# Sparse attention and an MLP on one core: products of zeros in TensorE's empty stretches, a third buffer of gathered values, two raw slots of the first weight, and a new order

## The chip, the cores and the metric

The kernel runs on one core of a Trainium2 chip, in one launch. The metric is device time in microseconds (us) from the start of the launch to its end; the number of a kernel is the median of several executions. The profile is of one execution. PE is TensorE, DVE is VectorE, ACT is ScalarE, POOL is GpSimd, and SP is SyncE, which here only issues DMA transfers.

## What is computed

Block-sparse attention over 4 batches, 8 heads, 768 positions and head size 64, and behind it a two-layer MLP over the 3072 tokens. A query block of 32 positions sees its own and both neighbouring key blocks, the first and the last block, and three sampled blocks; the first and the last query block see all keys. Cut down, the reference is:

```python
mask = abs(blk_i - blk_j) <= 1                      # 24 blocks of 32 positions
mask |= (blk_i == 0) | (blk_j == 0) | (blk_i == 23) | (blk_j == 23)
for qb in range(24):
    for kb in sampled_blocks[qb]:                   # three per query block
        mask[rows of qb, columns of kb] = True
attn = softmax(where(mask, q @ k.T / 8, -1e9)) @ v
x = attn, heads side by side                        # 3072 x 512
h = x @ w_in                                        # 512 x 2048
g = h * tanh(softplus(h))
out = g @ w_out                                     # 2048 x 512
```

Both weights arrive as 64-bit floats and are brought to a pair of f16 values (a high and a low part) on the chip.

## The kernel before, in words

**The jobs.** Each batch has 13 attention jobs: eleven pairs of query blocks, each block with gathered keys and values, and two dense jobs (first and last query block). They are numbered through from 0 to 51. A job is a chain over the engines: `s` (scores, PE, L633 for batch 0 and L643 for the others), `mx` (row maximum, DVE, L686), `nb` (L699 or L701), `pt` (exponentials, ACT, L712), `t` (transposes, PE, L732), `pp` (back to SBUF, ACT and DVE), `o` (product with the values, PE, L777 or L787), `r` and `xs` (division, DVE, L808 to L813), `tx` (transpose, PE, L820), `xh` and `xl` (two f16 parts, ACT and DVE, L838 and L841). Batch 0 is computed in f32, the others in pairs of f16.

**The gathers.** The values of a batch are written to a table in DRAM (`vd`, L527). For each query block SP issues transfers of the window (L590), of rows of zeros at the ends (L593) and of the three sampled blocks (L596) into a buffer `vg`. There are two such buffers (`NVG`), used in turn; a gather into a buffer waits until the `o` that reads it is done. Sampled keys are copied by POOL (`kg`, L574).

**The weights.** `w_in` comes in eight pieces of 1 MB into a ring of three raw slots (`wr`, L857). A piece is decoded by three DVE instructions (L865, L868, L871), then PE takes its squares (`gram_wi`, L357), and when two pieces are there a scale is found (`tp_w`, L381, and `ws`), and each piece is split into its high part (`wi`, L926) and low part (L929). `w_out` comes in sixteen pieces of 0.5 MB (`wor`) into the ring `raw` of six slots, which the raw tiles of Q, K and V of the coming batches use as well. It is decoded by the same three lines, squared (`gram_wo`), given one scale for all (`tp_wo`, L383), and split (L963, L966, L968).

**The MLP.** It works on twelve tiles of 256 tokens, three for each batch. A tile has 16 steps `h` of 12 products of 128x256 (L1007), taken from PSUM by ACT (`hs`, L1016), the activation on ACT, DVE and POOL (L1030 to L1051), and 16 steps `y` of 6 products of 128x512 (L1066). The first `h` step of a batch's first tile needs the jobs 0 to 4, and its split weights. The PSUM ring `h` has two slots; the squares of `w_in` use it too.

**The order.** Nothing of this is ordered by hand or at run time. Each step is added to a plan with an estimated length, what it reads and writes, which ring slots it takes, and a number (`key=`). `Plan.emit` walks through time, takes for each engine the step that could begin first, among those within 0.02 of each other the one with the lowest ready time plus `key`, and emits it. On an engine the instructions then run in that order, each waiting for its inputs, and whatever is behind a waiting instruction on the same engine waits as well. `pace` holds back the `s` of a job: the first eighteen by a list of earliest times (`START`), the later ones by how much of the MLP is done (`RES`).

Of the kernel before, what the change touches and what calls it, by code (L numbers as in the profile page):

```python
# [10 lines left out]
F16 = mybir.dt.float16  # L11
BF16 = mybir.dt.bfloat16
I32 = mybir.dt.int32
AF = mybir.ActivationFunctionType
# [11 lines left out]
RINGS = dict(s=1, t=2, o=1, h=2, y=1, raw=6, wr=3, pt=2, pp=4, xh=3, xl=3, mx=3, nb=3, r=2,  # L26
# [14 lines left out]
class Plan:  # L41
# [42 lines left out]

    def emit(self, pace):
# [16 lines left out]
        while todo:  # L102
# [30 lines left out]
            start, t, took, t.eng = best  # L133
            for e in t.ways:
                ready[e].remove(t)
# [42 lines left out]
def attn_mish_kernel(ctx: ExitStack, tc: tile.TileContext, qT, kT, v, sampled, blocks, w_in, w_out, out):  # L178
# [134 lines left out]
    NKG, NVG = 2, 2  # L313
# [45 lines left out]
    def add_gram(key, srcs, keys, ring, out, w, new_, cls):  # L359
# [7 lines left out]
        for n, k in enumerate(keys):  # L367
            add("PE", 0.45 if ring == "y" else 0.8, lambda n=n: fn(n), r=[k], w=[kg], new=[(ring, kg)] if n == 0 else (),
                key=cls + 3, lat=0.25)
# [4 lines left out]
        add("DVE", 0.4, diag, r=[kg], w=w, new=new_, key=cls - 7)  # L374
# [20 lines left out]
    def add_root(key, ss, fn, r, after, w, new, cls, n=1, apart=False):  # L395

        add("PE", 0.3 * n, lambda: root_pe(key, ss(), apart), r=r, w=[key], new=[("t", key)], key=cls + 4, lat=0.3)
        add("DVE", 0.6, fn, r=[key, *after], w=w, new=new, key=cls - 23)

    def load32(what, j):  # L400
# [4 lines left out]
        def fn():  # L405
# [5 lines left out]
            key=-23, lat=1.8, kind=("dma", 4.4 if what == "k" else 1.5, 1))  # L411

    def load(b, what, js, ring="raw", after=()):
# [3 lines left out]
        def fn():  # L417
# [12 lines left out]
            new=[(ring, key) for key in keys], key=-5 if b == 0 else 0, lat=1.8,  # L430
            kind=("dma", 1.5 * n, n))

    def sums(b, what, j, cls):
# [7 lines left out]
        add("ACT", 1.28, fn, r=[("raw", what, b, j)], w=[key], new=[(f"ss{what}", key)] if first else (), key=cls + 87)  # L441
# [24 lines left out]
    def parts(b, what, j, cls):  # L466
# [32 lines left out]
        if what == "v":  # L499
            add("POOL", 0.5, ends, w=[("ends",) + key], r=[kr], new=[("raw", key)], use=[key], key=cls - 5)  # L500
# [3 lines left out]
            use=use + ([key] if what != "k" else []), key=cls - 22)  # L504
        add("DVE", 1.3, lo, port=True, r=[kr, ks, kh], w=[key, ("done",) + key], use=use, key=cls + 3)

    def copy_v(j):
# [14 lines left out]
        add("POOL", 0.3, ends, w=[("ends",) + key], new=[("raw", key)], use=[key], key=21)  # L522
        add("DVE", 0.8, lambda: fn("DVE"), r=[kr, ("ends",) + key], w=[key], use=[key], key=ATV + 53,
            also=[("ACT", 1.16, lambda: fn("ACT")), ("POOL", 2.0, lambda: fn("POOL"))])

    def store_v(b, j):
        add("SP", 0.9, lambda: nc.sync.dma_start(  # L527
            out=vd[b][j * TT:(j + 1) * TT].rearrange("(c p) h d -> p c h d", p=P), in_=tl["v", b, j]),
            r=[("v", b, j)], w=[("vd", b, j)], key=37, lat=1.8, kind=("dma", 1.7, 1))
# [4 lines left out]
    def globals_(b):  # L534
# [5 lines left out]
        for n in range(NKG):  # L540
            add("POOL", 1.0, lambda n=n: fn(n), r=KT3(b), w=[("kg", n)], use=[("kt", b)], key=-7)

    def globals_v(b, n):
# [3 lines left out]
        add("SP", 0.9, fn, r=VD3(b), w=[("vg", n)], key=-1, lat=1.8, kind=("dma", 0.5, 2))  # L547
# [19 lines left out]
    def gather_k(su):  # L567
# [7 lines left out]
        add("POOL", 1.3, fn, r=KT3(b) + ["off"], w=[("kg", n)], use=[("kt", b)], key=10)  # L575
        if su["whole"]:
            add("DVE", 0.5, lambda: nc.vector.tensor_copy(  # L577
                out=kgs[n][:, :, 0:WK], in_=tl["kt", b][:, :, (qb - 1) * BS:(qb + 2) * BS]),
                r=KT3(b), w=[("kw", n)], use=[("kt", b)], key=-12)

    def gather_v(su):
# [15 lines left out]
        add("SP", 2.3, fn, r=VD3(b) + ["off", "z"], w=[("vg", n)], key=-16, lat=1.8, kind=("dma", 1.1, NR + 1 + (a0 > 0) + (a1 < WK)))  # L597

    def fetch_dense(su):
# [11 lines left out]
        for j in T3:  # L611
# [3 lines left out]
                key=8, lat=1.8, kind=("dma", 1.7, 1))  # L615
# [32 lines left out]
    def attend(job):  # L648
# [9 lines left out]
        def s_fn():  # L658
# [17 lines left out]
            use=[("kt", b)], key=104, lat=0.25, kind=("S", i))  # L676
# [12 lines left out]
        add("DVE", 2.6 if dense else 1.27, mx_fn, r=[ks] + (k2 if dense else []), w=[kmx], new=[("mx", kmx)], key=10.5)  # L689
# [4 lines left out]
        def nb_fn(eng):  # L694
# [9 lines left out]
            new=[("nb", ("nb", i))], key=-1.5, also=[("DVE", 0.35 * len(wq), lambda: nb_fn("DVE"))])  # L704
# [50 lines left out]
        for j in range(nt):  # L755
            kj = ("t", i, j)
            add("PE", 0.48, lambda j=j: t_fn(j), r=[("p", i, j // 2 if dense else j)], w=[kj, "t in order"], new=[("t", kj)], use=kps,
                key=10, lat=0.25, kind=("T", i))
            kpp = ("pp", i, j)
            if exact(b):  # L760
                add("ACT", 0.62, lambda j=j: pp_fn(j, "ACT"), r=[kj], w=[("ph", i, j), ("pl", i, j)], use=[kpp],
                    new=[("pp", kpp)], key=-2.5, also=[("DVE", 0.72, lambda j=j: pp_fn(j, "DVE"))])
                continue
            add("ACT", 0.62, lambda j=j: ph_fn(j), r=[kj], w=[("ph", i, j)], new=[("pp", kpp)], use=[kpp], key=-29.5)
# [515 lines left out]
```

## Time and profile before

| what | value |
|---|---|
| median of 3 runs | 774.58 us (773.07 to 776.49) |
| the profiled execution | 773.79 us |
| its span, first to last instruction | 772.0 us |
| PE busy, share of the span | 93% |
| DVE, ACT, POOL busy | 63%, 68%, 41% |
| bytes moved by DMA | 94.08 MB |

The span lies 1.8 us under the profiled execution's own time. A row of the timeline gives the start, the length, the engine, the line, the operation with the tile that it writes and those that it reads, and in brackets how long the engine had stood idle before it and for whom. The window view gives for each stretch the busy time of each engine, then the clock that PE was granted (1.00 is full), the share of time that the 16 DMA engines were busy, and GB/s. The chain of waits is followed back from the last instruction, at each step to what released it.

### The profile page before, as it was taken

Reading aid. Unit: us, or ns where it says so; the run is one execution under the profiler, and the core shown is the slowest. Engines: PE = TensorE matmul, PEld = TensorE weight load, DVE = VectorE, ACT = ScalarE, POOL = GpSimd, SP = SyncE. Lnnn points to the kernel's source line nnn. Section 1 sums busy time; section 2 is a strip of 40 time slices with the busy share of each in tenths; the row PEclk is TensorE's granted clock in tenths of the full one; section 3 lists DMA queues with packets and bytes.
Section 4 is the critical chain, followed back from the end, with each engine's and each line's share of the span. In section 5 each row is a group of like instructions: output and inputs, shape, how many; then the busy total and the mean of one; then the engine's idle time right before and its main releaser. Section 6 shows DMA issues by size and latency. Waiting matters only on the chain.

```text
span 772.0 us, 27811 instructions
## 1 busy us (share of the span) xinstructions
PE 714.2 (93%) x11766; PEld 501.7 (65%) x11766; DVE 486.2 (63%) x868; ACT 523.9 (68%) x811; POOL 314.1 (41%) x402
## 2 busy tenths in 40 slices
PE   2765888899999999999999999999999999999997
PEld 1554666565777666766677767677676676666663
DVE  3877988987867755767667767877766642323230
ACT  4455767888867777876677868777777665555650
POOL 2168531685436434434534534344551522213021
PEclk9768999999999999999999999999999999999999
DMA  7899796212524555154245643534333330000000
GB/s 274 303 279 231 219 261 211 82 43 98 180 59 119 159 142 154 66 167 117 58 113 143 180 138 103 160 89 127 99 86 93 117 88 15 14 15 14 14 15 28
DMA packets 55905, 94.08 MB, mean 122 GB/s; under 512 B 8035, under 2 KB 18788, under 8 KB 55780
## 3 DMA queue, kind: packets, MB, share of 16 engines
q1 hardware_dynamic: 55584, 92.03, 40.4%
q8 instruction: 93, 1.52, 0.9%
q14 instruction: 32, 0.26, 0.1%
q10 hardware_dynamic: 196, 0.27, 0.1%
HBM read 79.32 MB, written 12.95 MB: 120 GB/s over the span
## 4 chain that ended last, share of the span: by engine, by line
PE 78%; DMA 10%; DVE 6%; ACT 2%; issue 2%; SPq 1%; POOL 1%; POOLq 0%; ACTq 0%; DVEq 0%
PE y L1066 30%; PE h L1007 29%; DMA vg<-vd 7%; PE t L732 6%; PE o L787 5%; PE s L643 4%; PE tx L820 1%; PE o L777 1%; DMA q<-in_q_dram 1%; PE s L633 1%; POOL wo L968 1%; DMA wr<-in_moe_w_in_dram 1%; ACT pt L712 1%; DVE q L492 1%; DVE kg L577 1%
## 5 line engine op out<-in xcount | busy, mean ns | idle before, releaser
L1007 PE MATMUL h<-xh,wi 128*128 128x256 f16 x1536 | 282.4, 273 | 3.0 <-issue 1.6
L1066 PE MATMUL y<-wo,g 128*128 128x512 f16 x1152 | 277.9, 379 | 1.5 <-POOL g L1051 0.9
L1007 PEld LDWEIGHTS <-wi 128*128 128x128 f16 x2304 | 222.7, 98 | 54.3 <-issue 6.9
L1007 PE MATMUL h<-xl,wi 128*128 128x256 f16 x768 | 209.3, 273 | 0.2 <-issue 0.2
L1051 POOL TENSOR_TENSOR g<-hs,g 128x1024 f16<-128x1024 f32 x48 | 104.3, 2173 | 252.7 <-DVE g L1048 143.6
L1066 PEld LDWEIGHTS <-g 128*128 128x128 f16 x1152 | 110.6, 98 | 102.6 <-issue 3.7
L574 POOL COPY kg<-kt 128x256 f16 (+1 forms) x264 | 108.1, 453 | 88.0 <-PE s L643 57.0
L1016 ACT ACTIVATE hs<-h,gsc 128x512 f32<-128x512 f32 x96 | 65.6, 686 | 77.4 <-PE h L1007 77.4
L712 ACT ACTIVATE pt<-s,nb,ns 128x256 f32<-128x256 f32 (+1 forms) x208 | 104.5, 580 | 1.4 <-DVE nb L701 0.4
L1040 DVE SCALAR_TENSOR_TENSOR hs<-us,hs 128x1024 f32<-128x1024 f32 x48 | 60.6, 1263 | 53.4 <-ACT us L1039 53.3
L732 PE MATMUL t<-ident,pt 128*128 128x128 f32 x448 | 73.4, 288 | 9.3 <-ACT pt L712 8.4
L749 ACT ACTIVATE pp<-t 128x512 f16<-128x512 f32 x84 | 49.8, 595 | 39.6 <-PE t L732 38.7
L752 DVE SCALAR_TENSOR_TENSOR pp<-t,pp 128x512 f16<-128x512 f32 x84 | 57.1, 684 | 28.8 <-ACT pp L749 28.5
L732 PEld LDWEIGHTS t<-ident,pt 128*128 128x128 f32 x448 | 53.5, 146 | 21.7 <-issue 7.8
L1036 POOL TENSOR_TENSOR us<-us 128x1024 f32<-128x1024 f32 x20 | 38.6, 1932 | 60.9 <-DVE us L1034 50.8
L686 DVE TENSOR_REDUCE mx<-s 128x4 f32<-128x1024 f32 x44 | 53.3, 1212 | 6.4 <-PE s L643 3.8
L1030 ACT ACTIVATE us<-hs,hsc 128x1024 f32<-128x1024 f32 x48 | 55.2, 1150 | 1.2
L1038 ACT ACTIVATE us<-us 128x1024 f32<-128x1024 f32 x48 | 50.7, 1056 | 4.4 <-POOL us L1036 3.6
L1039 ACT ACTIVATE us<-us 128x1024 f32<-128x1024 f32 x48 | 50.8, 1058 | 1.0
L1034 DVE TENSOR_SCALAR us<-us 128x1024 f32<-128x1024 f32 x48 | 35.9, 747 | 22.6 <-ACT us L1030 22.3
L1048 DVE CAST g<-hs 128x1024 f16<-128x1024 f32 x37 | 28.9, 781 | 26.2 <-PE y L1066 25.6
L787 PEld LDWEIGHTS <-pp 128*32 128x32 f16 x4032 | 37.2, 94 | 12.0 <-issue 9.2
(188 smaller groups left out, 788.4 us busy)
## 6 DMA issues: line engine op xcount, KB each, us to landing
vg<-vd SPq DMA_DIRECT2D x304, 65.0 KB, 2.3
vg<-vd SPq DMA_DIRECT2D x80, 195.0 KB, 3.3
wr<-in_moe_w_in_dram SPq DMA_DIRECT2D x8, 1024.0 KB, 8.9
wor<-in_moe_w_out_dram SPq DMA_DIRECT2D x16, 512.0 KB, 4.4
vd<-v SPq DMA_DIRECT2D x12, 520.0 KB, 5.7
raw_v<-in_v_dram SPq DMA_DIRECT2D x12, 512.0 KB, 5.8
out_dram<-ys SPq DMA_DIRECT2D x24, 256.0 KB, 2.1
raw_k<-in_k_dram SPq DMA_DIRECT2D x9, 512.0 KB, 5.8
```

The lines of the kernel that those rows point to most:

```text
L574: nc.gpsimd.tensor_copy(out=kg[n][:, :, c0:c0 + BS], in_=kt[:, :, ds(j, BS)])
L686: nc.vector.tensor_reduce(out=mx.rearrange("p g w -> p (g w)"), in_=tl[ks].rearrange("p g (w k) -> p (g w) k", k=KT), axis=AX.X, op=ALU.max)
L712: ex = lambda o, x, g, w: nc.scalar.activation(out=o, in_=x, func=AF.Exp, bias=nb[:, g, w:w + 1], scale=ns(w)[:, 0:1])
L732: nc.tensor.transpose(t[:, k, g], src, ident)
L752: nc.vector.scalar_tensor_tensor(out=tl["pl", i, j], in0=tl["t", i, j], scalar=PSC, in1=tl["ph", i, j], op0=ALU.mult, op1=ALU.subtract)
L787: nc.tensor.matmul(o[cs, w, g, 0:v1 - v0], p[:, k, g, cs], vt[:, k, 2 * c + g, v0:v1], start=j == 0 and g == 0 and k == 0 and n == 0, stop ...
L1007: nc.tensor.matmul(h[:, f2].rearrange("p (s q) -> p s q", q=BS), wi[:, fp, w, cc, fs], x[:, :, cc], start=f2 == 0 and k == 0, stop=f2 == 1 ...
L1016: nc.scalar.activation(out=tl[kq][:, 2 * (fp % 2):2 * (fp % 2) + 2], in_=tl[kh], func=AF.Copy, scale=gsc[:, fp:fp + 1])
L1030: nc.scalar.activation(out=new(sb, "us", ku, [P, 4, TT]), in_=hs(), func=AF.Exp, scale=hsc[:, b:b + 1])
L1040: add("DVE", 1.32, lambda: nc.vector.scalar_tensor_tensor(out=hs(), in0=us(), scalar=-0.5, in1=hs(), op0=ALU.add, op1=ALU.mult), r=[ku], w ...
L1051: add("POOL", 2.3, lambda: nc.gpsimd.tensor_tensor(out=g()[:, 1], in0=hs(), in1=g()[:, 0], op=ALU.subtract), r=[kq, ("gh", b, t, k)], w=[k ...
L1066: nc.tensor.matmul(tl[ky], tl["g", b, t, k][:, g, f, q], wo[:, fc, w], start=fc == 0 and n == 0, stop=fc == NFC - 1 and n == 2)
```

## The change

Four things are changed.

- **Products of zeros.** `Plan.emit` looks, whenever it puts a step on PE whose estimated start lies between 3 and 150, at the estimated gap ahead of it. If it is over 0.5, it first emits `int((gap - 0.3) / 0.24)` matmuls of a 128x128 tile of zeros with itself, 512 columns wide (L860 in the changed kernel), into a PSUM tile that nobody reads. That tile is one of the two slots of the ring `h`, and is given back when job 8 (`LAST`), the ninth, begins. 97 such products are emitted.
- **A third `vg` buffer** (`NVG` 3). The dense job of a batch then has all three parts of its values in `vg`, and takes no slot of `raw`.
- **Two raw slots** of `w_in` in place of three.
- **The order.** Nearly all `key=` numbers, `START` and `RES` have other values.

```diff
-RINGS = dict(..., raw=6, wr=3, ...)
+RINGS = dict(..., raw=6, wr=2, ...)
...
+    zeros = None
+    FROM, TILL = 3.0, 150
...
             start, t, took, t.eng = best
+            idle = start - free.get("PE", 0.0)
+            if t.eng == "PE" and self.zeros and self.FROM < start < self.TILL and idle > 0.5:
+                self.zeros(int((idle - 0.3) / 0.24))
...
-    NKG, NVG = 2, 2
+    NKG, NVG = 2, 3
...
-            new=[(ring, key) for key in keys], key=-5 if b == 0 else 0, lat=1.8,
+            new=[(ring, key) for key in keys], key=(-5 if b == 0 else 0) + 90, lat=1.8,
...
+    z16 = const.tile([P, P], F16, name="z16")
+    nc.gpsimd.memset(z16, 0.0)
+    spare = []
+
+    def zeros(n):
+        for _ in range(n if spare else 0):
+            nc.tensor.matmul(spare[0].rearrange("p (n q) -> p n q", q=P), z16, z16.unsqueeze(1).to_broadcast([P, 4, P]),
+                             start=True, stop=True)
+
+    plan.zeros = zeros
...
+    LAST = 8
...
+    add("PE", 0.0, lambda: spare.append(new(ps["h"], "h", ("zeros",), [P, 512])), w=["zeros"], new=[("h", ("zeros",))],
+        key=-999)
...
+        if i == LAST:
+            add("PE", 0.0, spare.clear, r=["zeros", ("begun", i)], use=[("zeros",)], key=-1035)
...
-    RES, START = 1611, [82, 15, 81, 0, 10, 49, ...]
+    RES, START = 453, [218, 93, 2, 128, 14, 40, ...]
```

Three places show how instructions move. The first is SP at the first gathers. `wr` is a piece of `w_in`, `vg` a buffer of gathered values, `vd` the table in DRAM; L546 fetches the two fixed blocks, L590 opens a gather with the window. Before:

```order
L857 DMA wr_3_361<-in_moe_w_in_dram 128x4x512
L546 DMA vg0_111<-vd0_60 32x520 x2
L546 DMA vg1_112<-vd0_60 32x520 x2
L857 DMA wr_4_505<-in_moe_w_in_dram 128x4x512
L590 DMA vg0_111<-vd0_60 64x520
L593 DMA vg0_111<-vd0_60 32x520
```

The same place in the changed kernel:

```order
L873 DMA wr_4_544<-in_moe_w_in_dram 128x4x512
L552 DMA vg0_111<-vd0_60 32x520 x2
L552 DMA vg1_112<-vd0_60 32x520 x2
L552 DMA vg2_113<-vd0_60 32x520 x2
L873 DMA wr_5_657<-in_moe_w_in_dram 128x4x512
L596 DMA vg0_111<-vd0_60 64x520
L599 DMA vg0_111<-vd0_60 32x520
```

The first gather stood behind the piece with the number 4 and stands behind number 5 now; with two slots that piece waits until number 3 is decoded, as number 4 with three slots waited for number 1. Ahead of all this the two first pieces of `w_in` now stand before the three loads of V of batch 0, where they stood behind them. The second place is SP further on. Before, behind the fifth gather, the loads of K of batch 1 come (`raw_k_1`, three slots of `raw`):

```order
L596 DMA vg0_111<-vd0_60 32x520
L426 DMA raw_k_1_0_929<-in_k_dram 128x4x256
L426 DMA raw_k_1_1_931<-in_k_dram 128x4x256
L426 DMA raw_k_1_2_933<-in_k_dram 128x4x256
L590 DMA vg1_112<-vd0_60 96x520
```

In the changed kernel nothing but gathers stands between the eighth piece of `w_in` and the ninth gather, and behind that come pieces of `w_out` (`wor`):

```order
L602 DMA vg2_113<-vd0_60 32x520
L873 DMA wor_0_1277<-in_moe_w_out_dram 128x1024
L873 DMA wor_1_1296<-in_moe_w_out_dram 128x1024
L873 DMA wor_2_1304<-in_moe_w_out_dram 128x1024
L873 DMA wor_3_1346<-in_moe_w_out_dram 128x1024
L596 DMA vg0_111<-vd0_60 96x520
```

The loads of K and of the first Q of batch 1 have moved behind all sixteen pieces of `w_out`, the last of which stands nine SP rows ahead of the first of them. The third place is PE among the first jobs: `s_2` are the scores of job 2, `t_1` and `t_2` the transposes of jobs 1 and 2. Before:

```order
L732 MATMUL t_1_0_398<-ident_64,pt_1_372 128x128 x4
L732 MATMUL t_1_1_408<-ident_64,pt_1_372 128x128 x4
L820 MATMUL tx_0_416<-ident_64,xs_0_406 128x128
L633 MATMUL s_2_421<-kt_0_120,q_0_0_154 32x96 x8
L633 MATMUL s_2_421<-kg0_109,q_0_0_154 32x160 x8
```

In the changed kernel:

```order
L639 MATMUL s_2_477<-kg1_110,q_0_0_158 32x160 x8
L826 MATMUL tx_0_516<-ident_64,xs_0_513 128x128
L738 MATMUL t_1_0_534<-ident_64,pt_1_440 128x128 x4
L860 LDWEIGHTS z16_118
L860 MATMUL zeros_123<-z16_118 128x512
L860 LDWEIGHTS z16_118
L860 MATMUL zeros_123<-z16_118 128x512
L738 MATMUL t_1_1_553<-ident_64,pt_1_440 128x128 x4
```

The scores of job 2 went ahead of the transposes of job 1, and two products of zeros stand between those. 33 stand ahead of the first scores, 24 between these and the squares of the first piece of `w_in`, and the other 40 in 17 groups of one to five up to the start of job 8.

More of the change, by code (lines that the diff above doesn't have):

```diff
@@ L373, in diag @@
                                            accum_out=out())
-        add("DVE", 0.4, diag, r=[kg], w=w, new=new_, key=cls - 7)
+        add("DVE", 0.4, diag, r=[kg], w=w, new=new_, key=cls + 492)
     def root_pe(key, ss, apart):
@@ L395, in add_root @@
     def add_root(key, ss, fn, r, after, w, new, cls, n=1, apart=False):
[L397 to L398 removed]
+        add("PE", 0.3 * n, lambda: root_pe(key, ss(), apart), r=r, w=[key], new=[("t", key)], key=cls + 3, lat=0.3)
+        add("DVE", 0.6, fn, r=[key, *after], w=w, new=new, key=cls + 12)
     def load32(what, j):
@@ L440, in fn @@
             squares(tl["raw", what, b, j], tl[key][:, k:k + 1])
-        add("ACT", 1.28, fn, r=[("raw", what, b, j)], w=[key], new=[(f"ss{what}", key)] if first else (), key=cls + 87)
+        add("ACT", 1.28, fn, r=[("raw", what, b, j)], w=[key], new=[(f"ss{what}", key)] if first else (), key=cls - 74)
     def scales(b, what, j, cls):
@@ L499, in parts @@
         if what == "v":
-            add("POOL", 0.5, ends, w=[("ends",) + key], r=[kr], new=[("raw", key)], use=[key], key=cls - 5)
+            add("POOL", 0.5, ends, w=[("ends",) + key], r=[kr], new=[("raw", key)], use=[key], key=cls + 11)
         kh = ("hi",) + key
@@ L521, in fn @@
                 (nc.vector if eng == "DVE" else nc.gpsimd).tensor_copy(out=dst, in_=src)
-        add("POOL", 0.3, ends, w=[("ends",) + key], new=[("raw", key)], use=[key], key=21)
-        add("DVE", 0.8, lambda: fn("DVE"), r=[kr, ("ends",) + key], w=[key], use=[key], key=ATV + 53,
+        add("POOL", 0.3, ends, w=[("ends",) + key], new=[("raw", key)], use=[key], key=-2)
+        add("DVE", 0.8, lambda: fn("DVE"), r=[kr, ("ends",) + key], w=[key], use=[key], key=ATV - 63,
             also=[("ACT", 1.16, lambda: fn("ACT")), ("POOL", 2.0, lambda: fn("POOL"))])
@@ L977, in fn @@
             nc.vector.tensor_scalar(out=gsc, in0=iv_i, scalar1=rg, scalar2=-2.0 * GSC, op0=ALU.mult, op1=ALU.mult)
-        add("DVE", 0.7, fn, r=[("iv", k) for k in range(0, NFP, 2)], w=["gsc"], key=-14)
+        add("DVE", 0.7, fn, r=[("iv", k) for k in range(0, NFP, 2)], w=["gsc"], key=21)
     def scales_b(b):
```

90 lines of the change are left out of this document (45 added, 45 removed).

## The prediction

> **What bounds the kernel now.** I read the page first:
>
> ```profile
> span 772.0 us, 27811 instructions
> PE 714.2 (93%) x11766; PEld 501.7 (65%) x11766; DVE 486.2 (63%) x868; ACT 523.9 (68%) x811; POOL 314.1 (41%) x402
> ```
>
> PE is busy for 93% of the span, so over most of it a shorter wait elsewhere is worth nothing. Time can come only from the 57.8 us in which PE stands (772.0 - 714.2) and from where its clock is low. The window view says where that is; its columns are PE, weight loads, DVE, ACT, POOL, granted clock, DMA share and GB/s:
>
> ```profile
> 0.00:20.00 20.00, 6.03 (x102) 3.09 (x103) 7.56 (x26) 8.30 (x13) 5.61 (x26) 1.00 0.80 279
> 20.00:83.00 63.00, 44.31 (x924) 32.87 (x923) 50.57 (x96) 34.78 (x66) 34.81 (x49) 0.76 0.93 268
> 83.00:200.00 117.00, 103.00 (x1515) 74.85 (x1514) 101.11 (x158) 90.77 (x133) 62.26 (x60) 1.00 0.52 151
> 200.00:640.00 440.00, 433.39 (x8402) 309.79 (x8400) 295.93 (x552) 324.68 (x531) 184.89 (x256) 1.00 0.41 118
> 640.00:772.00 132.00, 127.47 (x832) 81.08 (x830) 31.04 (x37) 65.39 (x70) 26.50 (x12) 1.00 0.05 17
> ```
>
> PE stands for 14.0 us up to 20, 18.7 up to 83, 14.0 up to 200, and then 6.6 and 4.5; the clock is low from 20 to 83 alone. I cut at 83 because there the MLP begins, whose steps can fill PE. Three rows of PE's timeline, the second query block of job 1, that of job 4, and the first `h` product:
>
> ```profile
> 48.61 0.90 PE L777 MATMUL o<-vg,pp 128*32 128x65 f32 x32
> ...
> 78.06 0.66 PE L777 MATMUL o<-vg,pp 128*32 128x65 f32 x32
> ...
> 82.91 0.27 PE L1007 MATMUL h<-xh,wi 128*128 128x256 f16 x1
> ```
>
> What holds that up is in the chain of waits, in order of time:
>
> ```profile
> 40.41 7.62 DMA vg<-vd
> 48.05 6.61 DMA vg<-vd
> ...
> 63.49 7.60 DMA vg<-vd
> ...
> 72.49 1.89 PE s L633 x64
> ```
>
> From 40 to 71 nearly everything on the path is gathers: each goes out when an `o` has freed its buffer, and the next `o` waits for it to land. That is the stage in which a third buffer matters. In 20 to 83 DVE is the busiest engine, with 50.57 of 63 us, and stands for 12.4.
>
> **The gathers.** From 48.61 to 78.06 six query blocks pass, 4.9 us each, with two buffers in flight. With three, at the same latency, it is two thirds, 3.3 us, and six take 19.6 instead of 29.5: 9.8 us less. Is there bandwidth? The issue view has the sizes and the time to landing:
>
> ```profile
> vg<-vd SPq DMA_DIRECT2D x304, 65.0 KB, 2.3
> vg<-vd SPq DMA_DIRECT2D x80, 195.0 KB, 3.3
> wr<-in_moe_w_in_dram SPq DMA_DIRECT2D x8, 1024.0 KB, 8.9
> ```
>
> A gather is 195 + 3x65 = 390 KB, six are 2.3 MB, and two pieces of `w_in` go with them: 4.4 MB, at 268 GB/s 16 us, under 19.6. DVE allows up to 12.4 us, if it stood no more. It also waits less by its order: the decode of the last piece now stands ahead of job 3's division, behind which it stood:
>
> ```profile
> 72.55 0.22 DVE L808 TENSOR_SCALAR r<-o,iv_r 128x4 f32<-128x4 f32 x1 [3.06 <-PE o L777]
> ...
> 73.36 1.21 DVE L871 SCALAR_TENSOR_TENSOR wi<-wr,wi 128x1024 int32<-128x1024 int32 x1
> ```
>
> I take 9 us, with the ends 0 and 12.4. V of batch 0 now lands behind 2 MB of `w_in`, 7.5 us later at 279 GB/s, and with it the table that the gathers read. I cost that at nothing: before, the first gather was not held by V but stood on SP behind a piece of `w_in` that waited for a slot.
>
> ```profile
> 35.08 0.39 SPq L857 DMA_DIRECT2D wr<-in_moe_w_in_dram  x1
> 35.50 0.61 SPq L590 DMA_DIRECT2D vg<-vd  x1
> ```
>
> In the new order it stands behind another such piece, whose slot should come at about the same 35 to 40 us, since decoding begins earlier. Without that cover it costs up to 5 us.
>
> **Two slots of `w_in`.** A slot goes through landing (8.9 us) and decode (two DVE steps of 1.22 and a shorter one), about 12 us, so two slots give a piece every 6 us. From some 16 us on, the eighth is there at about 64, and the last decode before ended at 74.6. Nothing, while the gathers end later than that; if they don't, this is the next to be late.
>
> ```profile
> L868 DVE SCALAR_TENSOR_TENSOR wi<-wr,wi x8: 1207/1218/1941, 21.6 to 68.0; 128x1024 int32<-128x1024 int32 x8
> ```
>
> **K behind `w_out`.** By the tiles `raw_k` and `wor`, K of batch 1 was loaded at 58.8 and not taken until 175.2, and `w_out` was issued from 71.1 to 131.7:
>
> ```profile
> L426 SPq DMA_DIRECT2D raw_k<-in_k_dram x9: 413/505/1250, 58.8 to 421.5; - x9
> L488 ACT ACTIVATE kt<-raw_k,sc_k x9: 1132/1133/1151, 175.2 to 470.7; 128x1024 f16<-128x1024 f32 x9
> ...
> L857 SPq DMA_DIRECT2D wor<-in_moe_w_out_dram x16: 327/363/1582, 71.1 to 131.7; - x16
> L871 DVE SCALAR_TENSOR_TENSOR wo<-wor,wo x16: 677/692/710, 80.5 to 137.9; 128x512 int32<-128x512 int32 x16
> ```
>
> For all that time three of the six `raw` slots were taken, and `w_out` went through what was left. Now all are free for it, 2 MB less stands ahead of it, and K comes when it has passed. `y` can begin earlier than before (149.10, a row below). But PE stands only 14.0 us from 83 to 200, and much of this is attention waiting for gathers, so this is a gain of 0 to 14, and I take 4: `h` steps filled the time before `y`, and the splitting of `w_out` on POOL stays. The late K costs nothing as long as PE has `h` and `y` steps when job 13 should begin.
>
> **The zeros.** PE pays for them wherever it would not have stood. A product of that width takes 1.46/6 = 0.24 us at full clock, by the first row of `y`:
>
> ```profile
> 149.10 1.46 PE L1066 MATMUL y<-wo,g 128*128 128x512 f16 x6
> ```
>
> The launch is bounded by a POOL memset, ahead of which the tile of zeros is made, and by what the first scores wait for (us in total, times, longest):
>
> ```profile
> 1.43 0.52 POOL L294 MEMSET z<- 32x520 f32 x1
> ```
>
> ```profile
> PE s L633 <- DMA q<-in_q_dram: 9.5, 1, 9.5
> ```
>
> So 97 are 23.3 us, in stretches where PE stood 32.7. The 33 ahead of the first scores start at about 2 and take 7.9: they end when Q lands, at 9.5 to 10, or at 18 if each takes double. Job 0 can wait some microseconds, since V comes later. I take 1, between 0 and 8. The 40 behind take 9.6, placed by the plan's times and not by the chip's, beside 18.7 us of standing: I take 1, between 0 and 9.6.
>
> Their use would be the clock. In 20 to 83 it was 0.76 on average, so of 44.3 us of work 10.6 are stretch. The same 16 matmuls at a low and at the full clock:
>
> ```profile
> 29.49 0.57 PE L633 MATMUL s<-kt,q 64*32 64x96 f32 x16
> ...
> 79.99 0.40 PE L633 MATMUL s<-kt,q 64*32 64x96 f32 x16
> ```
>
> But PE is not what is waited for there. On the path lie some steps such as the 1.89 at 72.49; a full clock takes about 0.7 from each of four. DVE's 12.4 us cover both this and the gathers, so I add nothing for it.
>
> Against the zeros speaks this stretch, in which PE was busy 96% and had half the clock:
>
> ```profile
> 25.00:30.00 5.00, 4.78 (x73) 3.89 (x81) 4.45 (x14) 2.58 (x6) 0.00 (x0) 0.50 1.06 391
> ```
>
> The Trainium skill (TensorE: Matmul & The Clock Gate, Part 1) has a rule for it: the clock rises only after a window of about 3.4 us of sustained activity, and its Part 4 says that transposes don't count like other products. By that rule groups of one to five, 0.2 to 1.2 us, among transposes would not hold it, the 40 would cost up to 19.2 us instead of 9.6, and the sum would be that of the second case below. The row agrees so far as it goes; no run here shows zeros among them.
>
> **The middle.** From 200 to 640 PE stands 6.6 us. The order there is new as well, and jobs of batch 1 stand closer together on PE. I take 2 us more, between -4 and +20.
>
> **The sum.** -9 (gathers) - 4 (K behind `w_out`) + 1 + 1 (zeros) + 2 (middle) = -9. On the profiled execution's 773.8 this gives 764.8; the median of the runs shown, 774.58, lies 0.8 above it, so I forecast 765.6.
>
> **The other ways it can go.** *More than that:* if DVE hardly stands up to the first `h` product (-12) and PE stands half as long up to 200 (-7), with the other terms as they are, it is -15: 759.6 or a little under. For it speaks that both stages wait for transfers; against it, that DVE is busy 101 of 117 us from 83 to 200.
>
> *The zeros eat it:* the clock stays at half, each costs 0.48, the launch comes 8 us later, of which the later V hides half, and of the 19.2 us of the other 40 half stand in the way: -9 - 4 + 4 + 9.6 + 2 = +2.6, 777.2. For it speaks the row above; against it, that PE stood 32.7 us in those stretches.
>
> *The gathers are held on SP:* the first stands behind piece 5, the third behind 6, the fifth behind 7, and each of these waits for a decode. If decoding begins no earlier than before, the first gather goes out at about 40.5 instead of 35.5, the third behind a further landing and decode at about 49, and the gain of the third buffer is used up: 0 - 4 + 1 + 1 + 2 = 0, 774.6. For it speaks that the first gather did wait in this way; against it, that the two first pieces are loaded earlier.
>
> *The middle comes apart (slower):* the row with most standing there is
>
> ```profile
> 260.00:280.00 20.00, 18.17 (x341) 12.64 (x341) 10.78 (x21) 13.05 (x24) 8.59 (x14) 1.00 0.58 160
> ```
>
> with 1.83 us in 20. If denser jobs make half of the 22 such stretches like it, PE stands 20 us instead of 6.6; with a gain of only 5 ahead, since the same engines are fuller there too, that is +8: 783. With that gain it decides from about 16 us of standing between 200 and 640 on. Against it: ACT, the fullest of the others, is busy 324.68 of 440 us, 74%.
>
> **How the numbers follow.** A measurement of this kernel can tell about 0.5% from no change, 3.9 us. The forecast has a chance of 0.58, with its terms between 757 and 770.5; the larger gain 0.07; the zeros 0.12; the gathers held 0.10; the middle 0.13. The first two are faster by over 0.5%, 0.65; the two in between count as the same, 0.22; the last is slower, 0.13. The range goes from 754, which takes in the larger gain and some of its spread, to 779, which takes in the zeros and the held gathers and leaves out most of the slower case and the ends of the others, together under 0.2.
>
> **What would show it.** Right: the first `h` product between 71 and 77, six `o` of the jobs 1 to 4 in about 20 us, the last decode of `w_out` before 130, the first `y` before 140, and the windows' standing from 83 to 200 at about 10 us. The zeros' share is right if each takes about 0.23, the granted clock in 20 to 80 is 0.9 or more, and the first scores begin before 11.5. Wrong: a first `h` product at 82 or later, gathers going out on SP right after pieces of `w_in` again and again, scores that begin at 15 or later, or PE standing more than 16 us between 200 and 640.

## The result, and the profile after

The changed kernel took 785.72 us (median of four runs, 783.31 to 787.84) beside 774.71 for the kernel before: 1.0158 times as long, 95% interval 1.0125 to 1.0191. Forecast were 765.6, with 779 as the upper end. The profiled execution took 784.33, with a span of 782.6 against 772.0. The window view of the changed kernel, with the columns and cuts of the prediction:

```profile
0.00:20.00 20.00, 18.31 (x169) 8.65 (x169) 11.27 (x30) 4.66 (x7) 4.62 (x23) 1.00 0.94 336
20.00:83.00 63.00, 47.62 (x990) 31.94 (x975) 52.24 (x91) 36.63 (x70) 34.20 (x52) 0.92 0.78 238
83.00:200.00 117.00, 106.31 (x1500) 77.56 (x1501) 97.19 (x163) 87.47 (x133) 62.68 (x61) 0.94 0.52 154
200.00:640.00 440.00, 427.98 (x7967) 302.54 (x7965) 290.18 (x522) 327.02 (x533) 180.79 (x251) 0.99 0.41 116
640.00:783.00 143.00, 137.79 (x1256) 88.75 (x1254) 39.14 (x55) 71.86 (x85) 26.49 (x12) 1.00 0.10 30
```

The last row is the quickest reading. At 640 us, PE had 137.79 us of work left instead of 127.47: 10.3 us behind, which is nearly all of the 10.6 of the span. Where it fell behind is in the rows above. PE stood 15.4, 10.7 and 12.0 us from 20 to 640, against 18.7, 14.0 and 6.6: better in the first two stages, worse in the third. And up to 83 us, much of what took the place of standing was zeros:

```profile
L860 PE MATMUL zeros<-z 128*128 128x512 f16 x97 | 27.9, 426 | 1.7 <-POOL z L855 1.7
```

13.23 us of these lie between 20 and 83, and 14.72 before 20. Yet the early stages did nearly what the prediction had asked of them, as far as events go. The second query block of job 1 and that of job 4, on PE's timeline:

```profile
50.16 0.66 PE L783 MATMUL o<-vg,pp 128*32 128x65 f32 x32
...
71.70 0.66 PE L783 MATMUL o<-vg,pp 128*32 128x65 f32 x32
```

Six blocks in 21.5 us, against 29.5. By the views of the tiles `h`, `y` and `wo`, the first `h` product came at 77.1 instead of 82.9, the first `y` product at 141.5 instead of 149.1, and the last decode of `w_out` at 125.4 instead of 137.9:

```profile
L1082 PE MATMUL y<-wo,g x1152: 376/379/634, 141.5 to 778.5; 128*128 128x512 f16 x192
...
L1023 PE MATMUL h<-xh,wi x1536: 269/273/421, 77.1 to 755.6; 128*128 128x256 f16 x192
...
L887 DVE SCALAR_TENSOR_TENSOR wo<-wor,wo x16: 678/684/2614, 81.2 to 125.4; 128x512 int32<-128x512 int32 x16
```

But at 200 us that lead was nearly gone. The window from 0 to 200 for the line of `y` alone has 114 products in the changed kernel against 108 before, and for `h` 423 in both. Six `y` products are about 1.5 us at the prediction's 0.24 each.

One of the signs that the prediction had named as wrong is there too: on SP, gathers go out right behind pieces of `w_in`. The first and the third, each behind the piece ahead of it:

```profile
38.97 0.38 SPq L873 DMA_DIRECT2D wr<-in_moe_w_in_dram  x1
39.39 0.61 SPq L596 DMA_DIRECT2D vg<-vd  x1
...
47.23 0.70 SPq L873 DMA_DIRECT2D wr<-in_moe_w_in_dram  x1
47.98 0.49 SPq L596 DMA_DIRECT2D vg<-vd  x1
```

The fifth goes out so at 56.53. Before, these three went out at 35.50, 44.30 and 55.50.

### The profile page after: what moved, and what is told of

Same layout as the page of the kernel before. It is cut to its first block, busy times and chain, and to the rows that moved or that the text cites. A ratio compares the mean times of both kernels' runs of the same rounds, so it can differ in the third digit from the quotient of the medians.

```text
span 782.6 us, 28007 instructions
## 1 busy us (share of the span) xinstructions
PE 738.0 (94%) x11863; PEld 509.4 (65%) x11863; DVE 490.0 (63%) x860; ACT 527.6 (67%) x824; POOL 308.8 (39%) x398
## 3 DMA queue, kind: packets, MB, share of 16 engines
q1 hardware_dynamic: 56352, 93.09, 40.5%
q8 instruction: 93, 1.52, 0.8%
## 4 chain that ended last, share of the span: by engine, by line
PE 69%; DMA 10%; DVE 9%; ACT 4%; issue 4%; SPq 3%; POOL 1%; POOLq 0%; DVEq 0%; ACTq 0%
PE y L1082 26%; PE h L1023 25%; PE t L738 5%; PE o L793 4%; PE s L649 3%; DMA vg<-vd 3%; DMA raw_q<-in_q_dram 3%; DMA raw_v<-in_v_dram 2%; PE o L783 2%; PE tx L826 1%; DVE wt L979 1%; DMA q<-in_q_dram 1%; DVE kg L583 1%; DMA vd<-v 1%; SPq L602 1%
## 5 line engine op out<-in xcount | busy, mean ns | idle before, releaser
L1023 PE MATMUL h<-xh,wi 128*128 128x256 f16 x1536 | 286.2, 275 | 0.3 <-ACT hs L1032 0.2
L1023 PEld LDWEIGHTS <-wi 128*128 128x128 f16 x2304 | 226.2, 99 | 51.4 <-issue 2.9
L580 POOL COPY kg<-kt 128x256 f16 (+1 forms) x264 | 110.8, 465 | 93.2 <-PE s L649 76.2
L718 ACT ACTIVATE pt<-s,nb,ns 128x256 f32<-128x256 f32 (+1 forms) x208 | 106.3, 582 | 0.9
L1056 DVE SCALAR_TENSOR_TENSOR hs<-us,hs 128x1024 f32<-128x1024 f32 x48 | 62.9, 1310 | 46.5 <-ACT us L1055 46.4
L1052 POOL TENSOR_TENSOR us<-us 128x1024 f32<-128x1024 f32 x18 | 35.4, 1969 | 44.1 <-DVE us L1050 33.1
L1050 DVE TENSOR_SCALAR us<-us 128x1024 f32<-128x1024 f32 x48 | 39.5, 822 | 13.7 <-ACT us L1046 13.5
L1064 DVE CAST g<-hs 128x1024 f16<-128x1024 f32 x36 | 28.8, 801 | 29.5 <-PE y L1082 28.9
```

The costliest lines, as they stand in the source:

```text
L580: nc.gpsimd.tensor_copy(out=kg[n][:, :, c0:c0 + BS], in_=kt[:, :, ds(j, BS)])
L718: ex = lambda o, x, g, w: nc.scalar.activation(out=o, in_=x, func=AF.Exp, bias=nb[:, g, w:w + 1], scale=ns(w)[:, 0:1])
L1023: nc.tensor.matmul(h[:, f2].rearrange("p (s q) -> p s q", q=BS), wi[:, fp, w, cc, fs], x[:, :, cc], start=f2 == 0 and k == 0, stop=f2 == 1 ...
L1056: add("DVE", 1.32, lambda: nc.vector.scalar_tensor_tensor(out=hs(), in0=us(), scalar=-0.5, in1=hs(), op0=ALU.add, op1=ALU.mult), r=[ku], w ...
```

## The experiments

Ratios are to the kernel before, run beside; the changed kernel has 1.0158 [1.0125, 1.0191].

### The zeros: none, only at launch, narrow ones

No product at all (first edit), and only the 33 ahead of the first scores (second edit, alone):

```diff
-        for _ in range(n if spare else 0):
+        for _ in range(0):
...
-    FROM, TILL = 3.0, 150
+    FROM, TILL = 3.0, 12
```

> The changed kernel in its own order, with the PSUM slot still held, but no product of zeros is emitted. Theory 1 (the zeros are in the way): their 27.95 us of PE are only partly covered by stands; it comes out 6 to 12 us under the changed kernel, 774 to 780. Theory 2 (the new order is what costs): the zeros fill stands and cost nothing; without them the granted clock in 20 to 83 falls back to about 0.76 and it is 784 to 790.

> The changed kernel with only the zeros whose planned place is before 12 us, so none among the jobs. Theory 1: the 40 zeros among the jobs (13.23 us) are what is in the way, and this comes out like the kernel without zeros or 1 to 2 us under it, 773 to 779. Theory 2: 783 to 789, since the order is the same. In both the first scores start at about 11.

Without zeros: 1.0070 [1.0034, 1.0107], median 781.2, between the ranges of the two theories. With the 33 at launch: 1.0058 [1.0018, 1.0098], 776.6, in that of theory 1. Ten executions of each went from 773.5 to 783.2 and from 771.8 to 781.9, so one trace of this order can lie some microseconds off. Both orders are that of the changed kernel, so events can be compared one by one. The tile view of `y` with zeros at launch only:

```profile
L1082 PE MATMUL y<-wo,g x1152: 376/379/634, 137.4 to 771.9; 128*128 128x512 f16 x192
```

The first `y` product is at 137.4, without any zeros at 137.7, with all of them at 141.5. A second trace of the launch-only order is the run with the old keys in the later part (below), which gives each engine the same instructions in the same order up to 226 us: there it is at 140.3. So the 33 at launch do nothing that can be told from this spread, and the other 64 put PE 1 to 4 us back at this point. The clock from 20 to 83 was 0.84 without zeros and 0.77 with those at launch, with the first `y` product at the same time: as far as that, the clock is not what PE's progress hangs on. Theory 1 holds, at a smaller price at this point than I had given it. And without the zeros the order is still not faster than before, so theory 2 has a part as well.

The 64 behind the launch with 128 columns instead of 512:

```diff
+            if len(calls) == 1:
...
+            else:
+                nc.tensor.matmul(spare[0][:, 0:P], z16, z16, start=True, stop=True)
```

> The changed kernel with the zeros behind the launch made of 128 columns instead of 512, the same number at the same places; each should take about 0.06 to 0.12 us instead of 0.33. If their length is in the way: 4 to 6 us under the changed kernel in the same call. If it is the clock that they keep up, and narrow ones keep it up less: the clock in 20 to 83 falls to about 0.84 and the time is that of the changed kernel within 3 us.

1.0137 [1.0067, 1.0207], median 782.3, beside 780.9 for the changed kernel run with it: the second case, though the interval is wide. The 40 between 20 and 83 took 0.16 us each, not 0.06 to 0.12; all 64 took 7.7 us, where the wide ones had taken 18.6. The window of this run from 20 to 83, and its first `y` product:

```profile
20.00:83.00 63.00, 48.62 (x1040) 37.70 (x1039) 51.91 (x91) 37.66 (x72) 33.32 (x53) 0.79 0.82 243
```

```profile
L1088 PE MATMUL y<-wo,g x1152: 376/379/634, 143.6 to 776.1; 128*128 128x512 f16 x192
```

The clock is 0.79 with narrow zeros, 0.92 with wide ones: these do hold it up. But with narrow ones the first `y` product was just as far back, or further. So the price of the zeros is not their length alone; what of it is their place in PE's queue, and what the clock gives back for the wide ones, these runs don't part.

### The changed kernel again, and with 25 zeros at launch

> The changed kernel itself once more, for a second trace. If the 3.80 us stand on "issue" in the scores at 27 us comes from the zeros ahead of it, it stands at the same place again, and so do the four on "issue" between 350 and 525. If those stands fall anywhere in an execution, they are at other places, with a sum between 3 and 13 us, and the times spread by as much: 776 to 788.

And with 25 zeros at launch instead of 33, the other 64 as they were:

```diff
-        for _ in range(n if spare else 0):
+        for _ in range((25 if len(calls) == 1 else n) if spare else 0):
```

> The changed kernel with 25 zeros at launch instead of 33 and the other 64 as they were; PE's instructions behind the launch stand 16 rows earlier. If the 3 to 4 us stand on "issue" at 27 us hangs on the place in the program, it is gone or elsewhere, PE is only 1 to 2 us behind the run with launch zeros alone at 200 us, and the time is 774 to 781. If it comes of the zeros ahead of it, it stays, with 4 us at 200 and 780 to 786.

1.0115 [1.0073, 1.0158] and 1.0125 [1.0101, 1.0149], medians 780.9 and 784.1. The stand on "issue" at 27 us came again in the second trace of the changed kernel (2.96 us instead of 3.80) and is gone with 25 zeros. Yet in both the first `y` product comes as late as before (141.6 and 141.2), and with 25 the time lies where I had put the case in which the stand stays. So it is not that stand by which the zeros cost.

What came out besides is shown by three rows of PE's timeline, for the changed kernel and for the one with eight zeros fewer. The count at the end of a row is what was left of a group of 48 score products or 96 `o` products when PE stood still:

```profile
387.32 0.39 PE L649 MATMUL s<-kg,q 64*32 64x256 f16 x9 [1.97 <-issue]
...
408.48 0.28 PE L793 MATMUL o<-vg,pp 128*32 128x65 f16 x13 [2.95 <-issue]
...
523.35 0.51 PE L649 MATMUL s<-kg,q 64*32 64x256 f16 x19 [1.70 <-issue]
```

```profile
386.85 0.28 PE L649 MATMUL s<-kg,q 64*32 64x256 f16 x1 [2.14 <-issue]
...
407.19 0.27 PE L793 MATMUL o<-vg,pp 128*32 128x64 f16 x5 [3.83 <-issue]
...
524.26 0.40 PE L649 MATMUL s<-kg,q 64*32 64x256 f16 x11 [1.64 <-issue]
```

9, 13 and 19 have become 1, 5 and 11: each stand falls eight products later in the group, as eight products stand fewer ahead of it. In the second trace of the changed kernel, and in that with narrow zeros, it is 9, 13 and 19 again, with 1.1 to 4.1 us each. These stands belong to a place in PE's program, not to an instruction and not to a moment. In the run with zeros at launch only none of the three is there; the one on "issue" that is over a microsecond there is 1.26.

The same eight fewer in the kernel with zeros at launch only:

```diff
-        for _ in range(n if spare else 0):
+        for _ in range(25 if spare else 0):
```

> The changed kernel with zeros at launch only, 25 of them instead of 33. The order is the same; PE's instructions stand 16 rows earlier. If the stands on "issue" hang on where an instruction lies in PE's program, they are at other places than in the run with 33, and the time can be anything from 774 to 784 without another cause, by the sum of these stands. If they hang on what runs at that time, they stay at 208 and 263 us with about 1.5 us, and the time is within 1 us of that run: 775 to 778.

1.0016 [0.9994, 1.0038], median 775.0. The interval overlaps with that of the run with 33. Its one trace is of its longest execution, 785.15, and nothing is read from it. But this run and the one before it were timed side by side and differ by the 64 zeros among the jobs alone: 775.0 against 784.1. That is the cleanest price of these zeros, 9 us.

### The order

The kernel before with the third buffer and two raw slots, planned anew by its old table:

```diff
-RINGS = dict(..., wr=3, ...)
+RINGS = dict(..., wr=2, ...)
...
-    NKG, NVG = 2, 2
+    NKG, NVG = 2, 3
```

> The kernel before with its own table of keys and pacing, with a third buffer of gathered values and two raw slots of the first weight, no zeros; the planner orders it anew by the same keys. As forecast, the third buffer gains about 9: 764 to 768. Rival (the transfers were covered, or the planner does not use the buffer): 772 to 777. Theory 2, that the new table is what costs, says nothing against either.

The same with the zeros as well, as in the diff of the change:

> The kernel before with its own table of keys and pacing, with all three features: zeros, third buffer, two raw slots. Theory 1 (zeros in the way): 6 to 12 us over the same kernel without zeros. Theory 2 (the new table costs): within 3 us of the same kernel without zeros, and 8 or more under the changed kernel, 778 or less.

1.0101 [1.0069, 1.0133] and 1.0509 [1.0439, 1.0579]. Both lie above every time that I had given them. With its old table the planner makes a slower order of the first two features and a much slower one of all three. The forecast for the buffer fell here, but the order had changed with it, so this did not settle it. The new table is better than the old one for this set of features (1.0158 against 1.0509): it isn't the new numbers as such that cost.

The kernel before, with its features and every key moved a little; the second run has 53 in place of 37:

```diff
+        key += 0.5 * (fn.__code__.co_firstlineno * 37 % 21 - 10)
         t = Task({eng: (dur, fn, port), ...
```

> The kernel before, features and pacing as they were, with every key of its table moved by between -5 and +5, a fixed amount for each line. If the order before was a point found by trial, any small step away loses: 778 to 786, like the third buffer alone. Rival (small keys do not matter, the loss of the other runs belongs to their features and their table): 771 to 777.

> The kernel before with every key moved by between -5 and +5, by other amounts than in the first such run. If the order before is a point found by trial: slower again, 778 to 790, with most of it lost between 200 and 640. Rival (the first was an unlucky draw): 771 to 777.

1.0137 [1.0091, 1.0183] and 1.0382 [1.0362, 1.0401], with all features as before. Shifts of the keys by at most 5, in a table where the change moves them by up to 499, cost 11 and 30 us. The second is far over the 778 to 790 expected, and only part of its loss lies where I had put it: PE stood 8.9 us more than before from 200 to 640, and 8.5 us more ahead of that. The last two windows of the first of these runs:

```profile
200.00:640.00 440.00, 429.61 (x8295) 307.99 (x8294) 291.46 (x557) 340.51 (x555) 178.60 (x261) 1.00 0.42 120
640.00:830.00 190.00, 138.91 (x1091) 89.45 (x1089) 41.80 (x52) 68.41 (x75) 25.59 (x12) 0.99 0.05 16
```

PE stood 10.4 us from 200 to 640, against 6.6, and had 138.91 us left.

The kernel with zeros at launch only, with the old keys in its later part (jobs from 18 on, MLP steps from the fifth on, the preparation of batch 2):

```diff
+    def K(new, old):
+        return old if late[0] else new
...
-            use=[("kt", b)], key=4, lat=0.25, kind=("S", i))
+            use=[("kt", b)], key=K(4, 104), lat=0.25, kind=("S", i))
```

> The changed kernel with the zeros at launch only, and with the old keys for the jobs from 18 on, for the steps of the MLP from the fifth on and for the preparation of batch 2; PE's order is the same up to about 220 us. Theory 2a (the early part gains its 6 us, and it is the new keys in the middle that lose 10 to 14): 764 to 770, and at 200 us PE is as far as in the run with launch zeros only. Rival (any order that was not tried out on the chip as a whole loses there, and the two halves do not fit together): 774 to 784.

1.0146 [1.0101, 1.0191], median 783.1: the rival. By the ratios, the same early order with the old keys behind it is slower than with the new ones (1.0058). PE stood 13.9 us from 200 to 640, and had 135.22 left at 640. The two traces show less of it: the spans are 3.9 us apart, and 2.9 of these are there at the first `y` product, where both orders are still the same.

### Each feature with the order held fixed

Here the planner plans as before, and only what the instructions use is changed; so each engine runs the same instructions in the same order, but for the zeros ahead of PE's first one and for one to four pairs of small transfers on SP that a third buffer needs.

The zeros at launch:

```diff
+    zt = new(ps["h"], "h", ("zeros",), [P, 512])
+    for _ in range(33):
+        nc.tensor.matmul(zt.rearrange(...), z16, ..., start=True, stop=True)
     plan.emit(pace)
```

> The kernel before, every engine's order as it was, with 33 products of zeros ahead of PE's first instruction and nothing else. If zeros at launch are free and do nothing: the scores begin at 10 to 11 and the time is 771 to 776, with the stands on "issue" (4.7 us in the trace of before) at other places, since every instruction of PE now stands 66 rows later. If they pay by the clock: 766 to 770. If they are in the way: 777 or more.

1.0018 [1.0000, 1.0037]. The scores begin at 11.7, and PE is level with the trace of before from about 110 to 200 us. Zeros at launch bring nothing, and cost 3 us at most.

Two raw slots:

```diff
-RINGS = dict(..., wr=3, ...)
+RINGS = dict(..., wr=2, ...)
...
-    plan = Plan(RINGS)
+    plan = Plan(dict(RINGS, wr=3))
```

> The kernel before, every engine's order as it was, with two raw slots of the first weight in memory instead of three and nothing else. As forecast (0): 772 to 776. Rival: the third load of that weight waits on SP for a decode and holds the gathers behind it, 777 or more.

1.0290 [1.0254, 1.0326], median 793.7: 21 us for a slot that I had costed at nothing. The view of waits of this run, one row each for SP's queue up to 130 us and for PE up to 200 (us in total, times, longest):

```profile
SPq L857 <- DVE wi L871: 22.1, 3, 9.4
```

```profile
PE o L777 <- DMA vg<-vd: 19.5, 13, 7.0
```

SP stands 22.1 us ahead of loads of `w_in` for DVE's decodes, where it was 1.6 before, and the gathers stand behind those loads on SP: PE waits 19.5 us for them up to 200, against

```profile
PE o L777 <- DMA vg<-vd: 8.6, 10, 2.4
```

before. In the changed kernel SP stood 8.3 us for such decodes, in its own order; that kernel with three slots was not run, so what the missing slot costs there is open.

The same with three buffers of gathered values in turn:

```diff
-            vg = (vg32 if exact(b) else vgs)[n]
+            vg = (vg32 if exact(b) else vgs)[su["ng"] % 3]
```

> The kernel before, every engine's instructions in the order they had (only SP writes the global blocks of the third buffer too, four pairs of transfers more), planned as for two buffers of gathered values and three raw slots, but with a third buffer in turn and two raw slots in memory. A gather thus waits for an older job. If the third buffer gains what was forecast and only the new order loses it: PE's 8.6 us for gathered values up to 200 us fall to 3 or less, and the time is 764 to 770. Rival (with the order unchanged SP's queue holds the gathers anyway, or something else is late next): 771 to 776.

1.0289 [1.0245, 1.0332]: beside the loads of `w_in` the third buffer does nothing.

The third buffer with all three raw slots, up to the twelfth gather:

```diff
+    vg32.append(heads32(wo[:, NFC - 3:NFC]...bitcast(F32)[:, 0:RAW]))
...
+    def slot(ng):
+        return ng % 3 if ng < 12 else ng % 2
-            vg = (vg32 if exact(b) else vgs)[n]
+            vg = (vg32 if exact(b) else vgs)[slot(su["ng"])]
```

> The kernel before, every engine's order as it was and with its three raw slots; up to the twelfth gather the gathered values go to three buffers in turn, the third of which lies where the last pieces of the second weight go later. If the third buffer gains what was forecast: PE's wait for gathered values up to 200 us falls from 8.6 to 3 or less, PE is 4 to 9 us ahead of the kernel before at 200 us, and since a lead or lag at 80 us stood unchanged at the end in the run with two raw slots, the time is 764 to 770. Rival (SP's queue holds the gathers behind pieces of the first weight, or the work of other engines is late next): PE is less than 2 us ahead at 200 us and the time is 771 to 775.

The same with the 33 zeros at launch:

> The same with 33 products of zeros ahead of PE's first instruction. If zeros at launch do nothing, as with the order before alone: within 2 us of the run without them. If the warm start counts as soon as the gathers come earlier: 2 to 4 us under it.

1.0016 [0.9997, 1.0036] and 0.9997 [0.9975, 1.0018]: the rival, in both. SP shows why. Its waits for `o` from 35 to 75 us, that is for a buffer, before and with the third one:

```profile
SPq L590 <- PE o L777: 3.2, 5, 1.2
```

```profile
SPq L602 <- PE o L783: 0.3, 1, 0.3
```

So 3 us is all that a free buffer had to give there. The windows of the third, fourth and seventh gather went out, before and with the third buffer (there the third and every third after it are called `wo` for their place):

```profile
44.30 0.32 SPq L590 DMA_DIRECT2D vg<-vd  x1
...
49.45 0.32 SPq L590 DMA_DIRECT2D vg<-vd  x1
...
65.14 0.32 SPq L590 DMA_DIRECT2D vg<-vd  x1
```

```profile
43.54 0.49 SPq L596 DMA_DIRECT2D wo<-vd  x1
...
48.30 0.49 SPq L596 DMA_DIRECT2D vg<-vd  x1
...
63.56 0.36 SPq L596 DMA_DIRECT2D vg<-vd  x1
```

The third buffer let them go 0.8, 1.2 and 1.6 us sooner. With zeros at launch in both, the same three went out at 42.75, 48.30 and 64.26 with the buffer and at 43.05, 48.28 and 64.31 without: at most 0.3 sooner. (The eighth and the ninth go 2.9 and 3.2 sooner, in the second pair 0.7 and 1.8.) SP hardly waits for `o` any more and still issues the windows at nearly the same times, so most of what held them is what stands ahead of them on SP. The six blocks of the prediction took 30.9 us with the buffer, 1.8 of them a stand on "issue", against 29.5:

```profile
47.93 1.08 PE L783 MATMUL o<-vg,pp 128*32 128x65 f32 x32
...
78.81 1.09 PE L783 MATMUL o<-vg,pp 128*32 128x65 f32 x32
```

PE's wait for gathered values up to 200 fell from 8.6 to 6.1 us (`vg` and `wo` together):

```profile
PE o L783 <- DMA wo<-vd: 3.7, 2, 2.7
PE o L783 <- DMA vg<-vd: 2.4, 7, 0.6
```

With zeros at launch in both it rose instead, from 8.4 to 10.6. And in the first of these traces PE was all the same 1.4 us behind the kernel before at 200 us, by the times of the same instructions.

The kernel with zeros at launch only, its gathers in two of its three buffers:

```diff
-            vg = (vg32 if exact(b) else vgs)[n]
+            vg = (vg32 if exact(b) else vgs)[su["ng"] % 2]
```

> The changed kernel with zeros at launch only, in its order, but its gathers use two of the three buffers in turn. If the third buffer is what gave the 6 us that this order has gained at 200 us: PE is 5 to 10 us behind the run with three there, and the time is 781 to 787. Rival (the gain comes of the order and the buffer does nothing): PE is within 2 us of it at 200 us, 774 to 779.

1.0464 [1.0394, 1.0534], but this run tells nothing of the buffer. In an order planned for three buffers, a gather can stand ahead of the `o` of two gathers earlier; with two in turn that `o` then takes the later block's values, and waits for that later gather. Part of the computation is replaced by another, with other waits.

## Why the prediction was wrong

**The gathers, -9.** The step that failed is the reading of the path: "each goes out when an `o` has freed its buffer, and the next `o` waits for it to land". The chain did run through `o` and gathers in turn, but a freed buffer was only the last of several things that a gather waited for: before, SP waited 3.2 us for `o` in all from 35 to 75, where the sum took 9. With the order fixed the buffer is worth 0 (1.0016 and 0.9997), and the third, fourth and seventh gather leave 0 to 1.6 us sooner. "The gathers are held on SP" was named, at 0.10, and its times fit: it put the first and the third gather at 40.5 and 49, and they went out at 39.39 and 47.98. In the changed kernel the six blocks all the same took 8 us less, close to the 9 taken, in another order on SP, DVE and PE. But PE's wait for gathers up to 200 us did not fall there:

```profile
PE o L783 <- DMA vg<-vd: 9.0, 9, 2.1
```

against 8.6 before. How much of the 8 us is the buffer's was not settled, since the one run for it replaces part of the computation.

**The lead was to be kept.** The sum takes an early gain for a gain at the end. With the order fixed, a large lag stayed: in the run with two raw slots PE was 19 us behind at 80 us by the same instructions, and 20 at the end. A small one need not: against the run with zeros at launch only, the first `y` product came 4.1 and 4.2 us later in the two traces of the changed kernel, and the last ones began 6.6 and 1.0 later. Between two orders it does not follow at all. A part of the changed kernel's lead of 5.8 us at the first `h` product was lost before 200: its clock there was 0.94, which in 106.31 us is 6.4 us of stretch by these figures, and 1.00 before.

**K behind `w_out`, -4.** `y` began 7.6 us earlier and the decodes ended 12.5 us earlier, as said. But Q of batch 1 moved with K, and I had costed that at nothing "as long as PE has `h` and `y` steps". On PE's timeline of the changed kernel, and of the one with zeros at launch only, the product that sums Q's squares stands in the way instead:

```profile
124.73 0.38 PE L389 MATMUL tp_q<-ss_q,ones 128*128 128x1 f32 x2 [1.85 <-ACT I-2173_2174 L354]
```

```profile
120.60 0.38 PE L389 MATMUL tp_q<-ss_q,ones 128*128 128x1 f32 x2 [4.71 <-ACT I-2109_2110 L354]
```

ACT squares Q, and Q was loaded from 116.3 on, against 74.3 before. And POOL split the last piece of `w_out` at 169.1, against 169.6: the end of that chain did not move at all.

**Two slots, 0.** In the order before they cost 21 us. I had reckoned the rate of pieces, six us each, and not what stands behind a waiting load on SP. In the changed order their price was not tried.

**The zeros, +1 and +1.** At launch 0 to 3 us. The 24 between the first scores and the squares of `w_in` have no term in the sum; they took 5.35 us, and in the run with narrow ones PE stood 3.49 us for DVE at that place, so most of them filled a gap. The 40 behind took 0.33 us each instead of 0.24. All 64 put PE 1 to 4 us back at the first `y` product, where I took 1. But at the end they cost 9 us side by side (784.1 against 775.0), and by the ratios of all the runs of this order, 1.0115 to 1.0158 with zeros among the jobs and 1.0016 to 1.0070 without, 3 to 11. So this term is mis-sized. What makes the price is open. Stands on "issue" after 200 us are in it, 7.0 to 11.3 us in the three traces with wide zeros among the jobs and 2.3 with zeros at launch only; but they are 7.6 without any zeros, so they hang on where PE's program falls (see the last section), and no run moved that alone in the changed kernel. The clock did rise to 0.92. The Trainium skill (TensorE: Matmul & The Clock Gate, Parts 1 and 4) had led me to doubt that small groups of zeros would hold it; the traces do not agree with that doubt (0.92, 0.89 and 0.94 in the three traces of this order with wide zeros). That PE's clock is not waited for there was right, as far as the two runs with 0.84 and 0.77 show.

**The middle, +2.** This is the other term of the wrong size. From 200 to 640 PE stood 12.0 us instead of 6.6, and its clock was 0.99, about 4 us of stretch in 428 by a figure rounded to a hundredth; with the early lead used up, PE left that stage 10.3 us behind. The slower rival's place was right, its mechanism mostly not: of the 5.4 us of added standing, where it had 13.4, 3.8 are on "issue" (8.5 instead of 4.7), not a matter of dense jobs. That its 783 lies near the result is chance. What the rest is I can't settle. The chain of waits gives a clue that I have not followed up: from 200 to 640 that of the kernel before holds no transfer, and that of the changed kernel goes over loads of Q and V for the coming batches, among them

```profile
279.71 7.72 DMA raw_v<-in_v_dram
...
349.14 4.79 DMA raw_q<-in_q_dram
```

The loads of Q are on it in each of the traces with zeros at launch only, without zeros, and of the changed kernel again, with 3 to 5 per cent of that stretch. No run gave these loads an earlier place. It isn't the new keys as such, since old keys lose there too. By the same window row PE stood 5.5 to 8.1 us from 200 to 640 in the six traces with the order of before, and 9.1 to 16.1 in all the others, but for 26.2 in the run whose gathers use two of three buffers. That the order before was found by trying many on the chip would explain it; no run here shows how it was found.

## What to carry to other kernels

A row "waits for a buffer" names only the last of the waits: hold the order fixed, give the buffer, and see how much earlier the transfer goes out, before building a sum on it. In a kernel whose order comes out of a planner's table, test a feature in the old order first, and count with a loss for a new order that has not itself been tried: 1.0 to 3.8 per cent in four such orders here, and 0.2 to 0.7 in the changed one without zeros among its jobs. Products put into the gaps of a plan were not free, though PE had stood in those stretches, and the clock that they held up did not pay for them.

## What was not expected of the hardware

PE stands on "issue" for 1 to 4 us at fixed places of its program. Three such stands moved by exactly eight products when eight products ahead of them were left out, and stood at the same places in each of three traces with the same program length. In the changed kernel those after 200 us all lie in groups of short products, 96 `o` products in about 1.0 us or 48 scores in as much, and are 8.7 us:

```profile
PE o L793 <- issue: 5.0, 4, 2.9
PE s L649 <- issue: 3.7, 2, 2.0
```

In the kernel before they are 4.7, and 2.4 of these lie at `h` and `y` products, so short products are not a condition. The traces tell what lies at these places. PE's program comes in packets of a queue of its own, by the page of the changed kernel 93 of them with 1.52 MB, that is 16,384 bytes each:

```profile
q8 instruction: 93, 1.52, 0.8%
```

PE has 23,936 rows there (products, weight loads and a few for semaphores), about 256 for each packet. The three stands shown above come behind 12738, 13505 and 17346 of these rows, in the changed kernel and in the one with eight zeros fewer alike: 49, 52 and 67 times 256, and 193 or 194 more. All the other stands on "issue" in these two traces and in that of the kernel before lie at a multiple of 256 and 193 or 194 too, and each ends 1.2 to 1.6 us after one of those packets has landed (those of the changed kernel at 387.32, 408.48 and 523.35 after packets that landed at 385.82, 406.95 and 521.93). So there PE waits for the next part of its program. That a run of short products uses up a part before the next has come would fit; it was not tried.

Products of 512 columns held the clock where as many of 128 columns did not, 0.92 against 0.79.
